# The first product of the output part cut into four row-tiled pieces inside the attention's last couple, in an attention and gated-FFN kernel on one core

## The chip, the cores and the metric

The kernel runs on one core of one Trainium2 chip. The metric is the device time of one execution in microseconds, lower is better. Times of the kernel before: 864.58 median of three runs (864.47 to 865.11).

## The reference

`x` is [1, 2048, 640]; there are 32 heads of 192 columns, and attention sees the last W = 512 rows of the caches. All inputs are bf16.

```python
xn = _layernorm(x)
q  = (xn @ wq) by heads;  k, v = the last 512 rows of k_cache, v_cache
p  = _softmax(q @ k.T * 192 ** -0.5)
s  = (p @ v, heads side by side: [2048, 6144]) @ wo          # wo: [6144, 640]
g  = _silu((_silu(xn @ w_gate) * (xn @ w_up)) @ w_down)
out = x + s * g
```

## The kernel before

The work runs in three parts. First the norm and the FFN, whose gate `g` is parked in DRAM (`g_d`). Then attention, 32 heads as 16 pairs, two pairs to a couple, four phases to a couple (32 phases in all); its outputs are transposed by DMA and parked in DRAM as `o_d`, by 16 tiles of 128 rows and 48 chunks of 128 head columns. Last the output part, `o @ wo` with the gate and the residual.

**A phase** handles two blocks of 512 query rows of one head pair. Its order on every engine is written by hand in a string of tokens, one string for each phase: `PHASES` for the common couples, `FIRST` and `LAST` for the first and last couple. `token()` turns each into instructions. A `<` in front means that the token belongs to the phase before, a `+` to the phase after. The tokens that matter here:

- `s0` to `s7` (`scores`, L1047): six matmuls of 64 rows by 512 columns into a pair of PSUM banks named `sc`, then one exponential on ACT (L1051) that writes `p_t`. There are two such pairs of banks, used in turn.
- `0a0`, `0a1`, `0b0`, `0b1`, `1a0` ... `1b1` (`context_unit`, `pv`, L1085): block 0 or 1, half a or b of it, first or second half of the unit: 16 matmuls of 193 columns, row-tiled: the lo and the hi 64 rows of the array work at the same time and write different banks. A digit after the point names the bank pair (`0` and `1` are `mm0` and `mm1`; `s` takes an `sc` pair). Between a unit's two halves the row tiles change banks, and the second half waits for a marker that POOL writes after the first (`turn_t`, L1063). After the second half DVE takes reciprocals (L1103) and scales into `O_b` (`O_last` for the last two blocks); a letter says who scales: `v` DVE alone (L1107), `a` ACT alone (L1113), none one half each. A DMA transpose on SP's queue follows, and `sp` (`spill`) writes the blocks to `o_d`.
- `RD RS RA RB RM RT` and the same with `J` (`q_group`, L990): products that make the next phase's q in groups of ten matmuls, with copies on ACT (`SIDE`, L1025), sums on DVE (L1028, L1038) and on POOL (L1032).
- `kc`, `kl`, `vl`, `wc` and others: k and v of the next couple; `bm0` to `bm3` (`b_sum`, L1165): quarters of the weight sum of M7; `as0`: its left-hand sum; `lA`, `lB` (`load_a`, L1178): a 768 KB quarter of `o_d` into `a_q` (A the first row pair, B the second; 0 to 3 are A11, A12, A21, A22); `xg`: rows of `x` and `g` for the end; `lM5`: a quarter of `wo`.

**The output part** takes the 16 row tiles in eight row pairs and computes each pair by seven products (a Strassen-like scheme, `M1` to `M7`) of 24 matmuls of 128 rows by 320 columns (`product`, L1201). `ORDER` interleaves the first two row pairs: M1 and M7 of pair 0, M1 and M7 of pair 1, then M2 of both, M5, M6, M4, M3; then the other pairs one by one. M7, M5, M6 and M3 take left-hand sums (`a_sum`, L1193, three buffers in rotation) and M7, M5, M6 and M4 weight sums (`b_sum`), all on DVE. M1 is copied out by ACT (`u`), M2 accumulates on top of M1's bank, and `finish` gates and adds the residual on DVE (L1222, L1223). SP issues all loads and stores in program order, and each waits for what it reads and overwrites, so a later load queues behind an earlier one that waits.

The last phase's token string, before:

```python
"s0 <0a1 <lA3 bm2 as0 s1 <1a0.1 s2 <1a1v s3 lB3 <1b0.0 s4 <1b1v s5 s6 <sp0 0a0.1 lB1 s7 0a1 bm3 0b0.s "
"0b1a 1a0.0 1b0.1 1a1a 1b1 <sp1 xg0",
```

Of the kernel before, what the change touches and what calls it, by code (L numbers as in the profile page):

```python
# [15 lines left out]
def kernel(  # L16
# [13 lines left out]
    nc = tc.nc  # L30
# [50 lines left out]
    def mm_tile(which=None):  # L81
        which = mm_next[0] if which is None else which
        mm_next[0] = 1 - which
        return mm_pool[0].tile([P, 2, 512], f32, name="mm", tag="mm%d" % which)
# [1084 lines left out]
    def load_a(n, q, cs=slice(0, KH), eng=nc.sync):  # L1169
        side, k = divmod(q, 2)  # L1170
        if (n, q) not in a_q:
            if n > 1:
                a_q[n, q] = a_q[n - 2, q]
            else:
                pool = pre if n == 0 and k == 0 else wide
                a_q[n, q] = pool.tile([P, KH, P], bf, name="a_q", tag="a_q%d%d" % (n, q))
        src = o_d[ROW_PAIRS[n][side], :, k * KH + cs.start : k * KH + cs.stop, :]
        eng.dma_start(out=a_q[n, q][:, cs, :], in_=src)  # L1178
# [16 lines left out]
    def product(n, m, ps, first=True):  # L1195
        at = a_s[n, m] if (n, m) in a_s else a_q[n, A_OF[m][0]]
        pss = ps if isinstance(ps, list) else [ps]
        w = HC // len(pss)
        for k, ps in enumerate(pss):
            for c in range(KH):  # L1200
                nc.tensor.matmul(  # L1201
                    ps[:, 0:w], at[:, c, :], b_w[m][:, c, k * w : (k + 1) * w],
                    start=(first and c == 0), stop=(c == KH - 1), skip_group_check=True,
                )
# [13 lines left out]
    def finish(n, side, k, s, in_psum=False):  # L1218

        t, cols = xg[n, side], slice(k * HC, (k + 1) * HC)  # L1220
        y = f_tile(n, 3) if in_psum else s
        nc.vector.tensor_tensor(y, s, t[:, 1, cols], ALU.mult)  # L1222
        nc.vector.tensor_tensor(t[:, 0, cols], y, t[:, 0, cols], ALU.add)  # L1223

    def store(n, side, cols=slice(0, D), eng=nc.sync):
        r = ROW_PAIRS[n][side]
        eng.dma_start(out=out2[r * P : (r + 1) * P, cols], in_=xg[n, side][:, 0, cols])

    V = nc.vector

    ORDER = [(n, m) for ms in ((M1, M7), (M2,), (M5,), (M6,), (M4,), (M3,)) for n in range(2) for m in ms]
    ORDER += [(n, m) for n in range(2, len(ROW_PAIRS)) for m in PRODUCTS]
    A_SUMS = [nm for nm in ORDER if len(A_OF[nm[1]]) == 3]

# [5 lines left out]
    def bank(n, name):  # L1240
        acc[n, name] = late[1].tile([P, 512], f32, name="acc")[:, 0:HC]
        return acc[n, name]

    def run(n, m):

        ahead = n + 2 < len(ROW_PAIRS)
        u, v, c = (f_tile(n, k) for k in range(3))
        if m == M1:
            ps = bank(n, "M1+M2")
            product(n, M1, ps)  # L1250
            nc.scalar.copy(u, ps)  # L1251
        elif m == M7:
            ps = bank(n, "M7+M4")
            product(n, M7, ps)
            nc.scalar.copy(v, ps)
        elif m == M2:
            ps = acc[n, "M1+M2"]
            product(n, M2, ps, first=False)
            finish(n, 0, 0, ps, in_psum=True)
            if (n, M3) == ORDER[-1]:  # L1260
                store(n, 0, slice(0, HC))
        elif m == M5:
            pss = [bank(n, "M5+M3"), bank(n, "M5+M3'")] if (n, M3) == ORDER[-1] else [bank(n, "M5+M3")]
            product(n, M5, pss)
            w = HC // len(pss)
            for k, ps in enumerate(pss):
                total(v[:, k * w : (k + 1) * w], ps[:, 0:w], v[:, k * w : (k + 1) * w])
        elif m == M6:
            ps = bank(n, "M6")
            product(n, M6, ps)  # L1270
            total(u, ps, u)
            total(v, u, v)
            finish(n, 1, 1, v)
            for q in (A11, A21) if ahead else ():
                load_a(n + 2, q)
        elif m == M4:
            ps = acc[n, "M7+M4"]
            product(n, M4, ps, first=False)
            total(c, ps, u)
            finish(n, 1, 0, c)  # L1280
            store(n, 1)
            if ahead:
                load_a(n + 2, A22)
        else:
            ps, t, last_cols = acc[n, "M5+M3"], xg[n, 0], slice(HC, D)
            if (n, m) == ORDER[-1]:
                total(u, u, t[:, 1, last_cols], ALU.mult)
                total(u, u, t[:, 0, last_cols])
                pss = [ps, acc[n, "M5+M3'"]]
                product(n, M3, pss, first=False)  # L1290
                w = HC // len(pss)
                for k, ps in enumerate(pss):
                    part, cols = slice(k * w, (k + 1) * w), slice(HC + k * w, HC + (k + 1) * w)
                    total(c[:, part], ps[:, 0:w], t[:, 1, cols], ALU.mult)
                    total(t[:, 0, cols], c[:, part], u[:, part])
                    store(n, 0, cols, (nc.sync, nc.scalar)[k])
            else:
                product(n, M3, ps, first=False)
                total(u, ps, u)
                finish(n, 0, 1, u)  # L1300
                store(n, 0)
            if ahead:
                load_a(n + 2, A12)
                load_xg(n + 2)
        if (n, m) in A_SUMS:
            k = A_SUMS.index((n, m)) + 3
            if k < len(A_SUMS):
                a_sum(*A_SUMS[k])

    FIRST = (  # L1310
# [20 lines left out]
    )  # L1331
    LAST = (
# [8 lines left out]
    )  # L1341
    COUPLES = NPAIR // 2
    PHASES_N = 4 * COUPLES
# [46 lines left out]
    def token(s, x):  # L1390
        nonlocal wide

        cp, ph = divmod(s, 4)
        if x[0].isdigit():
            context_unit(s, *x.split("."))
        elif x[0] == "s" and x[1].isdigit():
            scores(first_step(s) + int(x[1]) // KC, int(x[1]) % KC)
        elif x[:2] == "sp":
            spill(first_step(s) + int(x[2]))
        elif x[:2] in ("DG", "JG"):  # L1400
            q_diag(JOINT if x[0] == "J" else 1 if ph < 2 else 0, *x[2:])
        elif x[0] in "RJ":
            group_of(s, x[0])[x[1]](*x[2:])
        elif x[:2] in ("TT", "QQ"):
            k, j = (int(x[2]), 2) if x[0] == "T" else divmod(int(x[2]), 2)
            q_rows(first_step(s + 1) + k, j, int(x[3]))
        elif x == "ah":
            if s in AHEAD:
                what, *args = AHEAD[s]
                what(*args)  # L1410
        elif x[:2] == "vl":
            pr = 2 * cp + (1 if x[2] == "O" else 2 if s else 0)
            if pr < NPAIR:
                load_v(pr)
        elif x == "free":
            actx.close()
            wide = ctx.enter_context(tc.tile_pool(name="out_b", bufs=1, reuse_waits="tile"))
            O_last = wide.tile([P, 2, 4, 2, Dh], bf, name="O_last")
            O_late.extend(O_last[:, k, :, :, :] for k in range(2))
        elif x[:3] == "lM5":  # L1420
            n = int(x[3])
            load_b(M5, None, nc.sync, n * KH // 4, (n + 1) * KH // 4)
        elif x[0] == "l":
            load_a("AB".index(x[1]), int(x[2]))
        elif x[:2] == "xg":
            load_xg(int(x[2]))
        elif x[:2] == "bm":
            b_sum(M7, int(x[2]))
        elif x == "as0":
            a_sum(*A_SUMS[0])  # L1430
        else:
            what, n = (x[:-1], (int(x[-1]),)) if x[-1].isdigit() else (x, ())
            of_pair(s, what, n)
# [26 lines left out]
    for k, (n, m) in enumerate(ORDER):  # L1460
        run(n, m)
        for step in sums.get((n, m), ()):
            b_sum(*step)
        if k < 4:
            load_b(M3, late[0], nc.sync, k * KH // 4, (k + 1) * KH // 4)

# [29 lines left out]
```

## Time and profile before

| what | value |
|---|---|
| median of three runs | 864.58 us (864.47 to 865.11) |
| the profiled execution | 864.99 us; span of the core 863.2 us |
| granted clock of PE | 1.00 of full speed |
| busy share: PE, DVE, ACT, POOL | 99%, 71%, 54%, 19% |
| PE matmuls | 9805 recorded |
| DMA | 149.14 MB, mean 173 GB/s |
| first matmul of the output part | 677.10 us from the span's start |

The profile is of one execution. Times inside it count from the span's start. L1201 is line 1201 of the kernel; a group of instructions is named by its line, its engine, and what it writes and reads. "Idle before" is the idle time of that engine just before an instruction, and after the arrow stands who ended it. Matmul times are modelled to their end in the array, so two matmuls in flight overlap in the record.

### The profile page before, as it was taken

The numbers are of one execution on the slowest core, as the hardware profiler recorded it, in microseconds if no ns is written. First come the engines' busy times: TensorE is split into PE (matmuls) and PEld (weight loads), VectorE is DVE, ScalarE is ACT, GpSimd is POOL, SyncE is SP. The second block draws the span as 40 slices with busy tenths as digits, with TensorE's granted clock in tenths as the row PEclk, the third lists the DMA queues.
The fourth block names the chain that finished last, engine by engine and source line by source line (L and its number), as shares of the span: only waits on it lengthen the run. The fifth ranks groups of instructions, "written<-read, shape, count | busy, mean of one in ns | idle before, by whom it ended". The sixth has DMA issues, their size and how long they took to land.

```text
span 863.2 us, 23199 instructions
## 1 busy us (share of the span) xinstructions
PE 855.9 (99%) x9805; PEld 569.2 (66%) x9815; DVE 613.9 (71%) x1041; ACT 468.4 (54%) x644; POOL 167.0 (19%) x247
## 2 busy tenths in 40 slices
PE   8999999999999999999999999999999999999998
PEld 6456446576667667667667667667666777777776
DVE  6687987878777777777777777776755786565564
ACT  4474675667767767767767767767767400000000
POOL 0010000103333333333333333333321000000000
PEclk9999999999999999999999999999999999999999
DMA  9879413558877889989999978978998977645510
GB/s 294 174 143 212 72 40 107 132 93 164 183 143 167 195 164 204 222 160 208 208 171 195 230 135 173 196 167 194 155 227 230 265 250 232 236 154 182 174 46 17
DMA packets 271496, 149.14 MB, mean 173 GB/s; under 512 B 174112, under 2 KB 267296, under 8 KB 271392
## 3 DMA queue, kind: packets, MB, share of 16 engines
q1 hardware_dynamic: 270608, 147.01, 74.5%
q8 instruction: 77, 1.26, 0.6%
q10 hardware_dynamic: 784, 0.65, 0.3%
q14 instruction: 27, 0.22, 0.1%
HBM read 80.51 MB, written 30.41 MB: 128 GB/s over the span
## 4 chain that ended last, share of the span: by engine, by line
PE 98%; DMA 1%; ACT 0%; issue 0%; DVE 0%; SPq 0%; POOL 0%; ACTq 0%; POOLq 0%
PE acc L1201 21%; PE sc L1047 19%; PE mm L1085 14%; PE mm L990 12%; PE sc L990 7%; PE sc L394 5%; PE sc L1085 5%; PE mm L479 3%; PE mm L637 3%; PE sc L637 2%; PE sc L479 2%; PE mm L978 1%; PE sc L690 1%; DMA wg_sb<-in_B_w_gate_dram 1%; PE gu L394 0%
## 5 line engine op out<-in xcount | busy, mean ns | idle before, releaser
L1051 ACT ACTIVATE p_t<-sc 128x1024 bf16<-128x1024 f32 x256 | 258.2, 1023 | 89.4 <-PE sc L1047 88.4
L1047 PE MATMUL sc<-q_all,khat 64*128 64x512 bf16 x1536 | 206.4, 376 | 0.8 <-ACT O_b L1113 0.6
L1085 PEld LDWEIGHTS <-p_t 64*128 64x128 bf16 x4096 | 179.7, 94 | 36.6 <-POOL turn_t L1063 0.5
L1085 PE MATMUL mm<-V_p,p_t 64*128 64x193 bf16 x3008 | 157.4, 243 | 0.2
L990 PEld LDWEIGHTS <-w_all 64*128 64x128 f16 (+1 forms) x1540 | 86.2, 94 | 71.1 <-issue 0.5
L1047 PEld LDWEIGHTS <-khat 64*128 64x128 bf16 x1536 | 82.8, 94 | 56.4 <-issue 6.3
L1032 POOL TENSOR_TENSOR m_f<-m_f 128x1024 f32<-128x1024 f32 x44 | 105.3, 2394 | 42.4 <-DVE q_all L1028 28.4
L990 PE MATMUL mm<-xc,w_all 64*128 64x512 f16 x890 | 112.0, 376 | 0.0
L1028 DVE TENSOR_TENSOR q_all<-mm,m_f 128x1024 bf16<-128x1024 f32 x44 | 53.9, 1224 | 55.9 <-ACT m_f L1025 55.7
L1201 PE MATMUL acc<-b_w,a_q 128*128 128x320 bf16 (+1 forms) x576 | 81.8, 299 | 0.0
L1107 DVE TENSOR_TENSOR O_b<-mm,r 128x384 bf16<-128x384 f32 x151 | 78.3, 553 | 3.5 <-DVE r L1103 0.2
L1251 ACT COPY xc<-acc 128x320 f32<-128x320 f32 x8 | 3.4, 425 | 135.7 <-PE acc L1201 135.7
L1063 POOL MEMSET turn_t<- 128x1 f32 x128 | 12.7, 99 | 314.5 <-PE mm L1085 239.5
L1201 PEld LDWEIGHTS <-a_q 128*128 128x128 bf16 x576 | 56.3, 98 | 22.0 <-issue 0.2
L1201 PEld LDWEIGHTS <-q_all 128*128 128x128 f16 x552 | 52.7, 98 | 19.1
L1038 DVE TENSOR_TENSOR q_all<-mm,m_f 128x1024 bf16<-128x1024 f32 x44 | 53.7, 1220 | 12.2 <-POOL m_f L1032 5.9
L1201 PE MATMUL acc<-b_w,q_all 128*128 128x320 f16 (+2 forms) x432 | 58.1, 292 | 0.0
L1085 PE MATMUL sc<-V_p,p_t 64*128 64x193 bf16 x1088 | 53.7, 243 | 0.3 <-POOL turn_t L1063 0.3
L1103 DVE RECIPROCAL r<-mm 128x4 f32<-128x4 f32 x94 | 16.9, 179 | 51.0 <-PE mm L1085 50.8
L173 DVE TENSOR_TENSOR w_all<-wq_rows 64x640 f16<-64x640 bf16 x90 | 50.9, 617 | 0.5
L990 PE MATMUL sc<-xnT,w_all 64*128 64x512 bf16 x350 | 44.1, 376 | 0.0
L1025 ACT COPY m_f<-sc 128x1024 f32<-128x1024 f32 x35 | 35.4, 1012 | 13.3 <-PE sc L990 6.8
(173 smaller groups left out, 1028.5 us busy)
## 6 DMA issues: line engine op xcount, KB each, us to landing
o_d<-OT_b SPq DMA_DIRECT2D x64, 384.0 KB, 4.0
a_q<-o_d SPq DMA_DIRECT2D x32, 768.0 KB, 6.2
wq_rows<-in_A_wq_dram SPq DMA_DIRECT2D x16, 480.0 KB, 4.7
b_w<-in_A_wo_dram SPq DMA_DIRECT2D x16, 480.0 KB, 5.0
wq_rows<-in_A_wq_dram SPq DMA_DIRECT2D x30, 240.0 KB, 5.4
K_p<-in_A_k_cache_dram SPq DMA_DIRECT2D x32, 192.0 KB, 3.5
V_p<-in_A_v_cache_dram SPq DMA_DIRECT2D x32, 192.0 KB, 4.0
xc<-xnT SPq DMA_DIRECT2D x10, 320.0 KB, 4.6
```

The source lines that it names most:

```text
L173: nc.vector.tensor_tensor(slot_of(w_sum, r, at, to), x, y, op)
L394: nc.tensor.matmul(out, w_sb[:, c, f * P : (f + 1) * P], xnT[:, c, qc], start=(c == 0), stop=(c == NC - 1),)
L479: nc.tensor.matmul(ps, left[:, c, :], D_OF[m][:, c, :], start=(first and c == 0), stop=(c == KD - 1), skip_group_check=True,)
L990: nc.tensor.matmul(ps[:, h, :], ws[h][r, c, :], xs[h][r, c, :], start=(first and c == 0), stop=(c == NC - 1), skip_group_check=True,)
L1028: nc.vector.tensor_tensor(to[:, 1:3, :], st["ps"][:, :, :], m_f[:, 5:3:-1, :], ALU.add)
L1032: nc.gpsimd.tensor_tensor(SIDE, diag, SIDE, ALU.subtract)
L1038: nc.vector.tensor_tensor(to[:, 0:4:3, :], st["ps"][:, :, :], SIDE, ALU.add)
L1047: nc.tensor.matmul(sc[:, h, :], khat[r, j, ks], q_of(i, j)[r, :], start=(j == 0), stop=(j == 2))
L1051: nc.scalar.activation(p_t[:, :, :], sc[:, :, :], ACT.Exp, scale=scale)
L1085: m = nc.tensor.matmul(acc[:, k, h * 256 : h * 256 + Dh + 1], Ps[i][kc][r, h, qt * P : (qt + 1) * P], V_of[i // NB % 2][r, kc, h, 0 : Dh + 1],
L1107: nc.vector.tensor_tensor(O_b[:, k, :, :], a_k[:, :, 0:Dh], r[:, k, :, :].to_broadcast([P, 2, Dh]), ALU.mult,)
L1201: nc.tensor.matmul(ps[:, 0:w], at[:, c, :], b_w[m][:, c, k * w : (k + 1) * w], start=(first and c == 0), stop=(c == KH - 1), skip_group_ch ...
```

## The change

M1 of row pair 0 leaves `ORDER`. Its work is done by the new function `first_product`, in four pieces `o0` to `o3` among the last phase's scores and context units: six chunks a piece, each chunk as two matmuls of 64 rows (lo and hi) that write the two banks of `mm1`. After the last piece ACT copies one bank to `u`, and DVE adds the other. M2 of pair 0 gets a bank of its own instead of M1's, and `u` is added to it by DVE. All four token strings of the last couple are new: `vlO`, `lM5`, the `bm` sums, `xg1`, the `lA` and `lB` loads and the context units stand in other places and partly in other banks. In the output part the left-hand sum for (1, M5) is issued after M1 of pair 1 and its weight sums, and a later pair's A12 is loaded with A22 after M4, ahead of the store, not after M3.

```diff
--- before.py
+++ after.py
@@ -1228,7 +1228,7 @@
 
     V = nc.vector
 
-    ORDER = [(n, m) for ms in ((M1, M7), (M2,), (M5,), (M6,), (M4,), (M3,)) for n in range(2) for m in ms]
+    ORDER = [(n, m) for ms in ((M1, M7), (M2,), (M5,), (M6,), (M4,), (M3,)) for n in range(2) for m in ms][1:]
     ORDER += [(n, m) for n in range(2, len(ROW_PAIRS)) for m in PRODUCTS]
     A_SUMS = [nm for nm in ORDER if len(A_OF[nm[1]]) == 3]
 
@@ -1240,6 +1240,21 @@
     def bank(n, name):
         acc[n, name] = late[1].tile([P, 512], f32, name="acc")[:, 0:HC]
         return acc[n, name]
+
+    def first_product(part):
+
+        if part == 0:
+            acc[0, "M1"] = mm_tile(1)[:, :, 0:HC]
+        ps = acc[0, "M1"]
+        for c in range(part * KH // 4, (part + 1) * KH // 4):
+            for h, r in enumerate((lo, hi)):
+                nc.tensor.matmul(
+                    ps[:, h, :], a_q[0, A11][r, c, :], b_w[M1][r, c, :], start=(c == 0), stop=(c == KH - 1),
+                    skip_group_check=True,
+                )
+        if part == 3:
+            nc.scalar.copy(f_tile(0, 0), ps[:, 0, :])
+            total(f_tile(0, 0), ps[:, 1, :], f_tile(0, 0))
 
     def run(n, m):
 
@@ -1254,9 +1269,11 @@
             product(n, M7, ps)
             nc.scalar.copy(v, ps)
         elif m == M2:
-            ps = acc[n, "M1+M2"]
-            product(n, M2, ps, first=False)
-            finish(n, 0, 0, ps, in_psum=True)
+            ps = acc[n, "M1+M2"] if n else bank(n, "M2")
+            product(n, M2, ps, first=n == 0)
+            if n == 0:
+                total(f_tile(n, 3), ps, u)
+            finish(n, 0, 0, ps if n else f_tile(n, 3), in_psum=n > 0)
             if (n, M3) == ORDER[-1]:
                 store(n, 0, slice(0, HC))
         elif m == M5:
@@ -1278,9 +1295,9 @@
             product(n, M4, ps, first=False)
             total(c, ps, u)
             finish(n, 1, 0, c)
+            for q in (A12, A22) if ahead else ():
+                load_a(n + 2, q)
             store(n, 1)
-            if ahead:
-                load_a(n + 2, A22)
         else:
             ps, t, last_cols = acc[n, "M5+M3"], xg[n, 0], slice(HC, D)
             if (n, m) == ORDER[-1]:
@@ -1300,11 +1317,10 @@
                 finish(n, 0, 1, u)
                 store(n, 0)
             if ahead:
-                load_a(n + 2, A12)
                 load_xg(n + 2)
         if (n, m) in A_SUMS:
             k = A_SUMS.index((n, m)) + 3
-            if k < len(A_SUMS):
+            if 3 < k < len(A_SUMS):
                 a_sum(*A_SUMS[k])
 
     FIRST = (
@@ -1330,14 +1346,14 @@
         "1a0.1 <sp0",
     )
     LAST = (
-        "s0 ah RD kcO0 kcO1 kcO2 kcO3 s1 <1a1v RSs kcO4 s2 +++xg1 RA <sp0 <1b0.1 s3 RB <1b1 s4 vlO RM +++lM50 +++lM51 +++lM52 +++lM53 "
-        "RT s5 0a0.1 s6 0a1v s7 +RD +RSs 1a0.s 0b0.1 +RA +RB 1a1v 0b1v",
-        "s0 RM <<sp1 s1 s2 JD s3 RT JS0 <1b0.s ah ++bm0 s4 <1b1a JA 0a0.0 0b0.s 0a1 0b1 JB s5 <sp1 JM s6 +RD "
-        "JT s7 +RS1 ++bm1 <sp0 +RA",
-        "s0 <1a0.s ah <1b0.1 <sp0 <1a1 <1b1 s1 RB s2 RM free s3 lB2 s4 <sp1 0b0.1 RT lB0 s5 0b1v lA1 s6 s7 "
-        "0a0.0",
-        "s0 <0a1 <lA3 bm2 as0 s1 <1a0.1 s2 <1a1v s3 lB3 <1b0.0 s4 <1b1v s5 s6 <sp0 0a0.1 lB1 s7 0a1 bm3 0b0.s "
-        "0b1a 1a0.0 1b0.1 1a1a 1b1 <sp1 xg0",
+        "kcO0 kcO1 s0 <1a1v s1 kcO2 RD s2 RSs <sp0 RA <1b0.1 s3 <1b1v s4 RB vlO s5 kcO3 RM s6 0a0.1 s7 RT ah "
+        "0a1a kcO4 0b0.s +++lM50 +RD +RSs 0b1 1a0.1",
+        "s0 ah RA <1a1 s1 ++xg1 ++lM52 RB RM s2 RT JD JSs ++bm0 JA s3 ++lM53 <1b0.0 JB s4 <1b1v s5 <<sp1 JM "
+        "0a0.s JT s6 +RD <sp1 0a1 +RSs 0b0.1 ++lM51 s7 +RA",
+        "s0 RB <0b1v s1 RM <1b0.1 RT s2 s3 <1b1v ah <1a0.0 s4 <1a1v <<sp0 <sp0 +bm1 s5 0a0.1 s6 0a1v s7 free "
+        "0b0.0 <sp1",
+        "s0 <0b1v s1 <1a0.1 s2 <1a1 <1b0.0 s3 as0 <1b1v <lB0 o0 s4 s5 o1 <lB2 <lA3 0a0.0 <lA1 lB3 bm2 s6 o2 "
+        "s7 0b0.s xg0 o3 0b1a lB1 1a0.s <sp1 bm3 1b0.1 1a1v 1b1 <sp0 0a1a",
     )
     COUPLES = NPAIR // 2
     PHASES_N = 4 * COUPLES
@@ -1426,6 +1442,8 @@
             load_xg(int(x[2]))
         elif x[:2] == "bm":
             b_sum(M7, int(x[2]))
+        elif x[0] == "o":
+            first_product(int(x[1]))
         elif x == "as0":
             a_sum(*A_SUMS[0])
         else:
@@ -1461,6 +1479,8 @@
         run(n, m)
         for step in sums.get((n, m), ()):
             b_sum(*step)
+        if (n, m) == (1, M1):
+            a_sum(*A_SUMS[3])
         if k < 4:
             load_b(M3, late[0], nc.sync, k * KH // 4, (k + 1) * KH // 4)
```

## The prediction

> **What bounds the kernel now.** I read the page first, then PE's waits, then the engine timeline of the last couple, the chain there, and the windows around it.
>
> The page says that the time is PE's work with almost nothing between:
>
> ```profile
> PE 855.9 (99%) x9805; PEld 569.2 (66%) x9815; DVE 613.9 (71%) x1041; ACT 468.4 (54%) x644; POOL 167.0 (19%) x247
> PEclk9999999999999999999999999999999999999999
> PE 98%; DMA 1%; ACT 0%; issue 0%; DVE 0%; SPq 0%; POOL 0%; ACTq 0%; POOLq 0%
> ```
>
> An edit that leaves PE's work as it is can only win the time in which PE stands, and the windows say where that is near the change (columns: the stretch, its length, busy time of PE, PEld, DVE, ACT, POOL, then clock, DMA share, GB/s):
>
> ```profile
> 640.00:660.00 20.00, 19.22 (x290) 13.22 (x288) 8.81 (x14) 15.21 (x25) 5.24 (x8) 1.00 0.70 165
> 660.00:680.00 20.00, 19.55 (x318) 14.93 (x314) 11.87 (x22) 15.54 (x25) 0.69 (x7) 1.00 1.10 298
> 680.00:700.00 20.00, 20.00 (x149) 14.41 (x148) 17.31 (x17) 1.70 (x4) 0.00 (x0) 1.00 1.01 266
> ```
>
> The output part from 680 on is full; the couple before it loses 0.78 + 0.45 us. The true loss is larger, since a matmul's last stretch through the array counts as busy. So I measure from start to start, in the timeline of PE:
>
> ```profile
> 653.44 0.83 PE L1047 MATMUL sc<-q_all,khat 64*128 64x512 bf16 x6
> 654.91 0.82 PE L1047 MATMUL sc<-q_all,khat 64*128 64x512 bf16 x6 [0.64 <-ACT O_b L1113]
> 655.56 1.26 PE L990 MATMUL mm<-xc,w_all 64*128 64x512 f16 x10
> 658.01 1.16 PE L1085 MATMUL mm<-V_p,p_t 64*128 64x193 bf16 x16
> 659.00 0.81 PE L1047 MATMUL sc<-q_all,khat 64*128 64x512 bf16 x6
> 665.58 0.85 PE L1085 MATMUL mm<-V_p,p_t 64*128 64x193 bf16 x16
> 666.60 0.82 PE L1047 MATMUL sc<-q_all,khat 64*128 64x512 bf16 x6 [0.18 <-ACT p_t L1051]
> 672.54 0.84 PE L1085 MATMUL sc<-V_p,p_t 64*128 64x193 bf16 x16
> 673.66 0.84 PE L1085 MATMUL sc<-V_p,p_t 64*128 64x193 bf16 x16 [0.28 <-POOL turn_t L1063]
> 677.10 1.12 PE L1201 MATMUL acc<-b_w,a_q 128*128 128x320 bf16 x7
> ```
>
> Undisturbed, a block of scores (6 matmuls) takes 0.65 from its start to the next one's (654.91 to 655.56), half a context unit (16) 0.667 (32 in 1.33 us), ten products of L990 1.08. Against these the starts slip by 654.91 - 653.44 - 0.65 = 0.82; 659.00 - 658.01 - 0.667 = 0.32; 666.60 - 665.58 - 0.667 = 0.35; 673.66 - 672.54 - 0.667 = 0.45; and by 0.15 at 646.68, 0.07 at 657.3 and 0.10 at 677.10 (four halves from 674.34 end at 677.01). **Sum: 2.26 us.** The first four are a score that waits for ACT to empty its PSUM pair after a context unit had it; two that wait for an exponential held up behind ACT's O_b scaling; and a half that waits for POOL's turn marker because its sister half stands right before it.
>
> **The change, part by part.**
>
> *PE's work.* The same scores, halves and products of q remain, in another order. M1 of row pair 0 leaves the output part: 24 matmuls of 128 rows. Six M1, M7 and M2 products run from 677.10 to 696.67, so one costs 19.57/6 = 3.26 us, 136 ns a matmul. It comes back as 24 pairs of 64-row matmuls. No row shows such a pair at 320 columns; a pair of 193 columns takes 0.667/8 = 83.3 ns, one of 512 takes 0.647/3 = 215.8, and the straight line between gives 136.0 at 320. So 24 x 136.0 = 3.26: no change. Bounds: -0.1 and +0.2, from the fit; halves that do not overlap are excluded by both rows. That line leaves 3 ns for a pair beyond its columns, so 24 more matmul instructions cost under 0.1 us. The Trainium skill ("TensorEngine Tiling (Array Packing)", Instruction Overhead) speaks against such a split: it gives each matmul some 60 cycles of overhead. Read as time added, at its 2.4 GHz, that is an estimate of 24 x 25 ns = 0.6 us and a forecast of 863.5; the 193-column row, with 3 ns a pair, does not agree.
>
> *What fills the gaps.* The q.k bank rule can be read from the rows: a block of scores ends on PE 0.18 after its last issue, ACT starts 0.04 later, takes 1.02, and PE wakes 0.05 after that: 1.29 us from the end of one block to the start of the next on the same pair of banks. With two pairs, the other block (0.65) and one half (0.667) cover it with 0.02 to spare. An O_b scaling on ACT (0.73) between needs one half more. A piece of M1 is six pairs, 0.82 us of PE with nothing behind it for ACT or DVE: a better filler than a half. Walking the last phase as written: s6 stands 2.1 us behind s4; 0b0.s finds s6's exponential done after o2 and s7 (1.47 against 1.29: 0.18 to spare); o3 stands between 0b0 and 0b1, so POOL's 0.45 is covered; no score there waits. 0.35 + 0.45 go. In the three phases before, with the new order alone, I find two places that fall short, both round the SIDE copy of phase 29: s3 waits 0.11 for an sc pair that ACT's two O_b scalings (0.73) free late, and s4 then waits 0.26 for the copy (1.01) that stood behind them. So 0.15 + 0.82 + 0.07 + 0.32 go, and 0.37 come. The 0.10 at the first full product stays.
>
> *Late starts.* The chain shows delays of 0.25 to 0.5 with nothing to wait for:
>
> ```profile
> 653.64 0.49 issue
> 654.13 0.74 ACT O_b L1113 x2
> 664.03 0.24 issue
> 664.27 0.57 DVE O_b L1107
> ```
>
> With plain durations the old order's slips add up to 1.65; the other 0.6 are these. They hurt only where there is little to spare; the new order has eight such places (0.02 to 0.29). I take 0.1; bounds 0 and 0.6.
>
> *What is added.* ACT's copy of one half of M1 (0.42, the row of L1251) waits for o3, and O_last's scalings queue behind it; DVE's add (0.49, as L1222) waits for the copy, and behind it stand a reciprocal and the fourth M7 sum (1.15). 1b0 needs mm1 back: 0.22 + 0.43 + 0.54 + 0.05 = 1.24 after o3, against 1.33 for the two halves between. The M7 sum ends some 2.6 after o3; the first full product comes six halves (4.0) after. Nothing, if the 0.09 holds; if not, a tenth or two. M2 of pair 0 gets one more DVE add (0.49): DVE is free by the time, nobody waits.
>
> *The cover that goes.* The output part begins with M7, and M1's 3.26 no longer stand before the sums. DVE's a_sum for (1, M7) ended 2.5 us after 677.10; needed 6.5 after. M5's sums ended 8.5 after; needed 16.3. The a_sum for (0, M6) ended 16.1 after; needed 22.8. All covered.
>
> *Queues.* A12 of a row pair is loaded before the store and with A22, one product earlier than now: SP's order loosens. In the last couple SP gets five a_q loads in a row, xg of pair 0, a transpose of O_last, then the sixth a_q; before, the six lay between 659.39 and 672.73, among transposes. See the rivals.
>
> *Sum* against the profiled execution (864.99; span 863.2 and 1.8 around it): -2.26 + 0.10 + 0.37 + 0.1 = -1.69, so 863.30. The median of the runs shown is 0.41 under that execution: 864.58 - 1.69 = **862.9**.
>
> **The rivals.**
>
> *Forecast*: 862.9; with no late starts and the two new waits gone 862.3, with 0.6 of late starts and 0.2 on the pairs 863.6.
>
> *The order brings its own waits.* The pieces fill only the last phase, where 0.80 was lost; 1.36 lay before it, where only the new order acts. For: the margins there are down to 0.02. Against: the walk. Gain 0.8: 863.8.
>
> *A held pair of banks.* From o0 to the add M1 holds mm1, so context units fall on mm0 and sc. If 0b0.s and 1a0.s each make PE wait like the 0.82 at 654.91, the gain is gone: 864.58 - 1.69 + 1.64 = 864.5. The Trainium skill (the same page, Gotcha 1: PSUM Pressure) warns of this: row tiles must write different banks. The 0.82 row agrees that a held pair can stop PE; the 0.18 to spare speaks against it here.
>
> *Slower: the sixth load.* A12 of pair 1 (lB1) now stands on SP behind five loads, xg and a transpose. From the first of the five, some 8.1 us before the first full product (11.2 of PE work after 1b1v, less 3 for its scaling and transpose), 6 x 0.786 + 0.66 + 0.2 = 5.6 MB must come; M2 of pair 1 wants it 13.05 after that product begins, so 21.1 in all. That needs 265 GB/s. The window 660 to 680 had 298 (18.8: 2.3 to spare); 640 to 660 had 165, at a DMA share of 0.70, so not for want of rate. At 216, the rate of the window 620 to 640 (DMA share 1.05), it takes 25.9, PE waits 4.8, and the time is 867.7. It is slower than before from 246 GB/s down. For: the loads begin later than now. Against: the landing of a_q was 9.6 us at worst in that stretch.
>
> **How the numbers follow.** Forecast 0.72, own waits 0.10, held pair 0.06, sixth load 0.12. About 0.2% (1.73 us, to 862.85) is what a measurement of this kernel can tell. The forecast's 862.9 lies at that bound, with the late starts unsure either way: 0.40 of its 0.72 I put below. The rest, 0.32, and the two middle rivals are within: 0.48. Slower: 0.12. The range takes in the forecast's bounds and the two middle rivals, 862.3 to 864.8, and leaves out the sixth load.
>
> **What would show it.** PE's starts in the last couple without slips of 0.3 and more, its waits there under 0.6 in sum; o0 to o3 each 0.82; the first full product 1.6 later than now (3.26 more work, 1.69 less standing), with the output part at 136 ns a matmul and no DMA named among PE's waits. It is wrong if a piece takes over 0.9, if PE waits for ACT O_b round 0b0.s, or if M2 of pair 1 waits for a DMA.

## The result, and the profile after

The changed kernel takes 862.55 us (median of 11 runs, 862.2 to 864.85) against 864.51 for the kernel before (11 runs, 864.12 to 865.31). The ratio is 0.998 with a 95% interval of 0.9971 to 0.9989. The medians lie 2.0 us apart, and the interval means 1.0 to 2.5 us faster. One execution of a version tested below (`0a1v`) took 1118.41 us at a granted clock of 0.75; it counts as slow and is left out of that version's ratio.

In the windows of the profile after (the stretch, its length, then busy time of PE, PEld, DVE, ACT, POOL, the clock, DMA share, GB/s) the last couple's idle time of 1.23 us is down to 0.10:

```profile
640.00:660.00 20.00, 19.90 (x300) 13.91 (x297) 11.68 (x20) 13.66 (x16) 5.30 (x8) 1.00 0.82 177
660.00:680.00 20.00, 20.00 (x340) 16.23 (x335) 11.47 (x23) 12.83 (x21) 0.69 (x7) 1.00 1.06 258
680.00:700.00 20.00, 20.00 (x149) 14.41 (x148) 19.90 (x21) 2.21 (x6) 0.00 (x0) 1.00 1.00 261
```

PE's waits in the whole execution now lie in the opening of the FFN alone; none for ACT O_b, p_t or POOL's marker is left:

```profile
PE gu L323 <- DVE q_all L267: 1.2, 1, 1.2
PE sc L394 <- DMA wg_sb<-in_B_w_gate_dram: 0.4, 1, 0.4
PE sc L394 <- ACT xnT L742: 0.2, 1, 0.2
```

The timeline of PE in the profile after shows the pieces (L1251) among the last phase, start to start without a slip, and the first full product:

```profile
666.87 0.99 PE L1251 MATMUL mm<-b_w,a_q 64*128 64x320 bf16 x12
667.68 1.48 PE L1047 MATMUL sc<-q_all,khat 64*128 64x512 bf16 x12
668.98 0.99 PE L1251 MATMUL mm<-b_w,a_q 64*128 64x320 bf16 x12
669.79 0.85 PE L1085 MATMUL mm<-V_p,p_t 64*128 64x193 bf16 x16
...
673.24 0.99 PE L1251 MATMUL mm<-b_w,a_q 64*128 64x320 bf16 x12
674.05 1.51 PE L1085 MATMUL sc<-V_p,p_t 64*128 64x193 bf16 x32
...
676.72 1.51 PE L1085 MATMUL mm<-V_p,p_t 64*128 64x193 bf16 x32
678.16 3.43 PE L1201 MATMUL acc<-b_w,q_all 128*128 128x320 f16 x24
```

A piece costs 667.68 - 666.87 = 0.81 us. Slips, counted as in the prediction from start to start, remain in three places: 0.20 at 648.45, 0.26 at 649.36, and 0.11 at the first full product. Sum 0.57, against 2.27 before (2.26 in the prediction, by rounding): 1.70 less. From the first full product to the end the kernel before took 863.2 - 677.1 = 186.1 us and the changed one 861.0 - 678.2 = 182.8, which is one product less and nothing else. So the other edits of the output part neither won nor lost time that can be seen here.

The span fell by 2.2 (863.2 to 861.0). Most of what the slips leave over lies ahead of the attention: the first 50 us, which the change does not touch, happen to have 0.4 more of PE busy (48.07 against 47.66), and the first exponential starts at 160.8 instead of 161.2. In the nine profiled executions of this document it starts between 160.2 and 161.2, latest in the kernel before, though none of the edits touches that part: this share of the gain is chance.

The two slips of 0.20 and 0.26 are one story, told by PE (first fence), DVE and ACT (second):

```profile
645.84 0.85 PE L1085 MATMUL sc<-V_p,p_t 64*128 64x193 bf16 x16
646.50 1.26 PE L990 MATMUL sc<-xnT,w_all 64*128 64x512 bf16 x10
647.58 0.84 PE L1085 MATMUL mm<-V_p,p_t 64*128 64x193 bf16 x16
648.45 1.73 PE L1047 MATMUL sc<-q_all,khat 64*128 64x512 bf16 x12
```

```profile
646.72 0.18 DVE L1103 RECIPROCAL r<-sc 128x4 f32<-128x4 f32 x1 [1.45 <-PE sc L1085]
646.94 0.56 DVE L1107 TENSOR_TENSOR O_b<-sc,r 128x384 bf16<-128x384 f32 x1
647.67 0.73 ACT L1113 ACTIVATE O_b<-sc,r 128x192 bf16<-128x192 f32 x2 [1.61 <-DVE O_b L1107]
648.29 1.01 ACT L1025 COPY m_f<-sc 128x1024 f32<-128x1024 f32 x1
649.31 1.02 ACT L1051 ACTIVATE p_t<-sc 128x1024 bf16<-128x1024 f32 x1
```

A context unit in an `sc` pair issues its last matmul just ahead of 646.50. Its scaling is split, one half on DVE and one on ACT, but the two run one after the other: DVE's half ends at 647.50, and ACT, which had been idle for 1.61 us, starts at 647.67. (In all 33 split units of this trace in which ACT stood idle when DVE's half ended, ACT began 0.08 to 0.17 behind that end.) So the pair is free only at 648.40, and the score due at 648.25 starts at 648.45. ACT's copy of the q product, behind that scaling, frees the other pair at 649.30, and the score due at 649.10 starts at 649.36.

SP's queue shows the six loads of `a_q` (first and last line) and the transpose ahead of the sixth:

```profile
670.19 2.84 SPq L1178 DMA_DIRECT2D a_q<-o_d  x5
...
677.17 4.36 SPq L1116 DMA_TRANSPOSE OT_b<-O_last  x1
681.58 0.63 SPq L1178 DMA_DIRECT2D a_q<-o_d  x1
```

The sixth landed at 689.82, and M2 of pair 1, which reads it, began at 691.21.

### The profile page after: what moved, and what is told of

It reads as the page before. It is cut to its first block, busy times and chain, and to the rows that moved or that the text cites. A ratio compares the mean times of both kernels' runs of the same rounds, so it can differ in the third digit from the quotient of the medians.

```text
span 861.0 us, 23263 instructions
## 1 busy us (share of the span) xinstructions
PE 855.7 (99%) x9839; PEld 569.5 (66%) x9839; DVE 616.8 (72%) x1046; ACT 466.7 (54%) x638; POOL 166.8 (19%) x247
## 4 chain that ended last, share of the span: by engine, by line
PE 98%; DMA 1%; ACT 0%; DVE 0%; SPq 0%; issue 0%; ACTq 0%
PE acc L1201 21%; PE sc L1047 19%; PE mm L1085 15%; PE mm L990 12%; PE sc L990 7%; PE sc L394 6%; PE sc L1085 5%; PE mm L479 3%; PE mm L637 3%; PE sc L637 2%; PE sc L479 2%; PE mm L978 1%; PE sc L690 1%; DMA wg_sb<-in_B_w_gate_dram 1%; PE gu L394 0%; PE mm L1251 0%
## 5 line engine op out<-in xcount | busy, mean ns | idle before, releaser
L1107 DVE TENSOR_TENSOR O_b<-mm,r 128x384 bf16<-128x384 f32 x155 | 80.3, 553 | 3.2
L1201 PE MATMUL acc<-b_w,a_q 128*128 128x320 bf16 (+1 forms) x552 | 78.4, 299 | 0.0
L1201 PEld LDWEIGHTS <-a_q 128*128 128x128 bf16 x552 | 54.0, 98 | 21.0
L1085 PE MATMUL sc<-V_p,p_t 64*128 64x193 bf16 x1056 | 51.9, 243 | 0.0
L990 PE MATMUL sc<-xnT,w_all 64*128 64x512 bf16 x370 | 46.6, 376 | 0.0
L1025 ACT COPY m_f<-sc 128x1024 f32<-128x1024 f32 x37 | 37.5, 1012 | 13.8 <-PE sc L990 7.3
```

Of the source, the lines that this page charges most:

```text
L990: nc.tensor.matmul(ps[:, h, :], ws[h][r, c, :], xs[h][r, c, :], start=(first and c == 0), stop=(c == NC - 1), skip_group_check=True,)
L1085: m = nc.tensor.matmul(acc[:, k, h * 256 : h * 256 + Dh + 1], Ps[i][kc][r, h, qt * P : (qt + 1) * P], V_of[i // NB % 2][r, kc, h, 0 : Dh + 1],
L1107: nc.vector.tensor_tensor(O_b[:, k, :, :], a_k[:, :, 0:Dh], r[:, k, :, :].to_broadcast([P, 2, Dh]), ALU.mult,)
L1201: nc.tensor.matmul(ps[:, 0:w], at[:, c, :], b_w[m][:, c, k * w : (k + 1) * w], start=(first and c == 0), stop=(c == KH - 1), skip_group_ch ...
```

## The experiments

"Slips" below are summed as above, over the last couple and the first product after it, in one profiled execution of each kernel. The kernel before has 2.27, the changed one 0.57. Slips recur: the pair of 0.20 and 0.26 stands in five of the kernels here, each time within 0.02 us. Ratios are to the kernel before, measured alongside. Of the versions that alter the changed kernel, only the one with the sixth load later has an interval clear of the changed kernel's; for the others the slips have to tell them apart.

**The new order without the pieces.** The kernel before with the four new strings, `o0` to `o3` left out (shown: the last phase's string):

```diff
-        "s0 <0a1 <lA3 bm2 as0 s1 <1a0.1 s2 <1a1v s3 lB3 <1b0.0 s4 <1b1v s5 s6 <sp0 0a0.1 lB1 s7 0a1 bm3 0b0.s "
-        "0b1a 1a0.0 1b0.1 1a1a 1b1 <sp1 xg0",
+        "s0 <0b1v s1 <1a0.1 s2 <1a1 <1b0.0 s3 as0 <1b1v <lB0 s4 s5 <lB2 <lA3 0a0.0 <lA1 lB3 bm2 s6 "
+        "s7 0b0.s xg0 0b1a lB1 1a0.s <sp1 bm3 1b0.1 1a1v 1b1 <sp0 0a1a",
```

> The kernel before with the new strings of the last couple alone, o0 to o3 taken out; M1 of pair 0 stays a full product in the output part. Theory 'order and pieces need each other': the two waits of the changed kernel round the SIDE copy stay (0.46 us), and without fillers the last phase walks to 1.7: s4 or s5 0.15 behind ACT's O_b scaling, 0a0 0.5 for DVE's scaling of 1b out of mm0, 0b0.s 0.65 for the exponential of s6 (0.65 of PE between instead of 1.29), 0b1 0.4 for POOL's marker right behind 0b0. Slips 2.2 to 2.4 in all, as many as before: 864.3 to 864.9, no gain. Rival 'the order wins by itself what lay ahead of the last phase': the last phase loses the old 0.8, slips 1.3: 863.5.

Measured: 864.38, the kernel before alongside 864.35, ratio 1.0001 (0.9992 to 1.001). Slips 2.30: the two of the changed kernel (0.20 and 0.25), then 0.14, 0.45, 0.70 and 0.46 in the last phase, 0.10 at the first product. In its timeline of PE:

```profile
668.50 0.84 PE L1085 MATMUL mm<-V_p,p_t 64*128 64x193 bf16 x16 [0.27 <-DVE O_b L1107]
669.17 1.46 PE L1047 MATMUL sc<-q_all,khat 64*128 64x512 bf16 x12
671.16 0.84 PE L1085 MATMUL sc<-V_p,p_t 64*128 64x193 bf16 x16 [0.53 <-ACT p_t L1051]
672.28 1.51 PE L1085 MATMUL sc<-V_p,p_t 64*128 64x193 bf16 x32 [0.28 <-POOL turn_t L1063]
```

The order alone wins nothing: what it saves ahead of the last phase (1.36 down to 0.45) it gives back there (0.80 up to 1.75).

**The pieces without the new order.** The changed kernel with the old strings, and in the last phase (a cut of the string):

```diff
-... <1b1v s5 s6 <sp0 0a0.1 lB1 s7 0a1 bm3 0b0.s 0b1a 1a0.0 ...
+... <1b1v o0 s5 s6 o1 <sp0 0a0.0 lB1 s7 o2 0a1 bm3 0b0.s o3 0b1a 1a0.0 ...
```

> The changed kernel with the old strings of the last couple, and o0 to o3 put into its last phase: o0 ahead of s5, o1 after s6, o2 after s7, o3 between 0b0 and 0b1. Theory 'order and pieces need each other': the fillers take away 0.45 (POOL's marker) and 0.2 to 0.35 at s5, the 1.36 ahead of the last phase stay: slips 1.5 to 1.75, 863.7 to 863.9. Rival 'the pieces are the whole gain': slips about 0.6, 862.6. Rival 'a held pair of banks costs': a new wait for ACT O_b or DVE in the last phase, 864.5 or more.

Measured: 863.98, ratio 0.9998 (0.9989 to 1.0007). Slips 1.82: POOL's 0.46 is gone, since `o3` now stands between the two halves (674.00 and 675.48), and all else is as before. One part missed: the 0.35 stayed, because that score is `s3` (665.65), and I put `o0` behind `s4`:

```profile
665.65 0.82 PE L1047 MATMUL sc<-q_all,khat 64*128 64x512 bf16 x6 [0.18 <-ACT p_t L1051]
666.30 0.84 PE L1085 MATMUL mm<-V_p,p_t 64*128 64x193 bf16 x16
666.96 0.83 PE L1047 MATMUL sc<-q_all,khat 64*128 64x512 bf16 x6
667.61 0.84 PE L1085 MATMUL mm<-V_p,p_t 64*128 64x193 bf16 x16
668.28 0.99 PE L1251 MATMUL mm<-b_w,a_q 64*128 64x320 bf16 x12
...
674.00 0.85 PE L1085 MATMUL sc<-V_p,p_t 64*128 64x193 bf16 x16
674.66 0.99 PE L1251 MATMUL mm<-b_w,a_q 64*128 64x320 bf16 x12
675.48 0.84 PE L1085 MATMUL sc<-V_p,p_t 64*128 64x193 bf16 x16
```

Both halves of the change together save 1.70; alone they save nothing and 0.45. The pieces are what lets the new order run.

**The pieces as full matmuls.** The changed kernel, M1 in the same four places but 128 rows high:

```diff
-            for h, r in enumerate((lo, hi)):
-                nc.tensor.matmul(
-                    ps[:, h, :], a_q[0, A11][r, c, :], b_w[M1][r, c, :], start=(c == 0), stop=(c == KH - 1),
+            nc.tensor.matmul(
+                ps[:, 0, :], a_q[0, A11][:, c, :], b_w[M1][:, c, :], start=(c == 0), stop=(c == KH - 1),
...
-            total(f_tile(0, 0), ps[:, 1, :], f_tile(0, 0))
```

> The changed kernel with M1's four pieces as full matmuls of 128 rows (six a piece, one bank, no DVE add) in the same places. Theory 'a change between 64-row and 128-row matmuls costs the 0.10 that stands at the first full product': eight such changes more, slips up by 0.8 from 0.6 to 1.4: 863.3, each piece 0.82 and about 0.1 lost ahead of it and behind it. Rival 'row tiling is beside the point, only the filler counts': slips as in the changed kernel, 862.5. Rival 'the split into 24 more matmuls costs 0.6': faster by up to 0.6, 862.0, pieces of 0.65 to 0.8.

Measured: 863.38, ratio 0.9988 (0.9979 to 0.9996). Slips 1.41. PE's waits name nobody in the last couple; the loss is round each piece, in the timelines of PE and of its weight loads (PEld):

```profile
665.55 0.85 PE L1085 MATMUL mm<-V_p,p_t 64*128 64x193 bf16 x16
666.33 0.99 PE L1250 MATMUL mm<-b_w,a_q 128*128 128x320 bf16 x6
667.25 1.47 PE L1047 MATMUL sc<-q_all,khat 64*128 64x512 bf16 x12
```

```profile
666.32 0.66 PEld L1250 LDWEIGHTS <-a_q 128*128 128x128 bf16 x6 [0.16 <-issue]
667.24 0.76 PEld L1047 LDWEIGHTS <-khat 64*128 64x128 bf16 x10 [0.26 <-issue]
```

From 665.55 a half ends its issue at 666.22, the piece starts at 666.33; its six matmuls (0.815) end their issue at 667.14, the scores start at 667.25: 0.11 each way. Over the eight changes it is 0.09 to 0.11 each, and the slips grow by 0.84. So the row tiling is worth that much, and the 0.11 at the first full product has the same size. The first weight load behind a change starts only with its matmul (666.32 and 666.33), and what holds it the profile doesn't name ("issue"). In the changed kernel the piece's first weight load starts at 666.79, 0.08 ahead of its matmul at 666.87. The Trainium skill ("TensorEngine Tiling (Array Packing)", Key Properties) says that a change of tiling mode drains the engine. The trace agrees with that as far as it goes: nothing of the next block starts early, and each change costs about 0.1 us.

**The two waits that are left.** The changed kernel with one token changed in the second string:

```diff
-... 0a0.s JT s6 +RD <sp1 0a1 +RSs 0b0.1 ...
+... 0a0.s JT s6 +RD <sp1 0a1v +RSs 0b0.1 ...
```

> The changed kernel with one token changed: unit 0a in an sc pair of the phase before the last but one is scaled by DVE alone, so that ACT's two O_b scalings (0.73) leave the way of the SIDE copy. Theory 'the two waits left come from ACT's O_b scaling in that queue': both go, slips 0.6 to 0.15, 862.1. Rival 'DVE becomes late instead': its two scalings (1.02 and a reciprocal of 0.18) free the sc pair later than ACT did, PE waits for DVE there, 862.5 or more.

Measured: 862.12, ratio to the kernel before 0.9976 (0.9966 to 0.9985). Slips 0.13, nearly all of it at the first full product. In the timelines of PE, DVE and ACT the two scores run without a gap:

```profile
647.88 0.84 PE L1085 MATMUL mm<-V_p,p_t 64*128 64x193 bf16 x16
648.54 1.48 PE L1047 MATMUL sc<-q_all,khat 64*128 64x512 bf16 x12
```

```profile
647.01 0.18 DVE L1103 RECIPROCAL r<-sc 128x4 f32<-128x4 f32 x1 [1.45 <-PE sc L1085]
647.23 1.02 DVE L1107 TENSOR_TENSOR O_b<-sc,r 128x384 bf16<-128x384 f32 x2
648.09 1.01 ACT L1025 COPY m_f<-sc 128x1024 f32<-128x1024 f32 x1 [1.74 <-PE sc L990]
```

The copy starts 0.20 earlier than in the changed kernel (648.29), though PE is 0.30 later here, so 0.50 earlier against PE's work. The rival failed because a split unit is not scaled side by side: DVE alone frees the pair 648.25 - 647.01 = 1.24 after its reciprocal begins, while half and half it took 648.40 - 646.72 = 1.68.

This version has the lowest median of all. Its interval overlaps the changed kernel's; that it is better by some 0.4 rests on the slips in the profile.

**The sixth load, later.** The changed kernel with `lB1` at the end of the last phase:

```diff
-... xg0 o3 0b1a lB1 1a0.s <sp1 bm3 1b0.1 1a1v 1b1 <sp0 0a1a
+... xg0 o3 0b1a 1a0.s <sp1 bm3 1b0.1 1a1v 1b1 <sp0 0a1a lB1
```

> The changed kernel with the sixth a_q load (A12 of pair 1) moved to the end of the last phase, so that it stands on SP behind all four O_last transposes. In the trace of the changed kernel it was issued at 681.58, landed at 689.82, and M2 of pair 1 began at 691.21: 1.4 us to spare; the fourth transpose was issued at 690.59 and took 1.42. Theory 'that load is the next thing to be late': issued about 691.3, landing 4 to 5 later, PE waits 3.5 to 5 ahead of M2 of pair 1 and nothing gives it back: 866.0 to 867.5, slower than before. Rival 'the DMA queues catch up': the transposes ahead go through sooner without the load between them, it lands by 692.5 and the wait is under 1.3: 862.5 to 863.8.

Measured: 867.68 (865.9 to 870.31), ratio 1.0032 (1.0018 to 1.0047): slower than before, and 0.2 above the upper end of what I expected. The profile is of the slowest of the eight executions, 870.31. There the load was issued at 691.98 and landed at 696.90; M2 of pair 1 was due at 692.69. In the timeline of PE, and in windows round it:

```profile
689.43 3.42 PE L1201 MATMUL acc<-b_w,a_q 128*128 128x320 bf16 x24
696.95 5.11 PE L1201 MATMUL acc<-b_w,a_q 128*128 128x320 bf16 x24 [4.09 <-DMA a_q<-o_d]
701.89 3.29 PE L1201 MATMUL acc<-xc,a_s 128*128 128x320 f16 x23
```

```profile
694.00:698.00 4.00, 1.05 (x8) 0.79 (x9) 3.93 (x5) 0.00 (x0) 0.00 (x0) 0.99 0.97 345
698.00:702.00 4.00, 4.00 (x19) 2.35 (x18) 0.15 (x1) 0.00 (x0) 0.00 (x0) 0.58 0.79 218
702.00:706.00 4.00, 4.00 (x32) 2.87 (x30) 2.63 (x5) 0.00 (x0) 0.00 (x0) 1.00 1.17 322
```

The wait, 696.95 - 692.69 = 4.3, lies where it was expected. What was not: the product behind it took 701.89 - 696.95 = 4.94 instead of 3.26, and the window 698 to 702 has a granted clock of 0.58. The slow stretch is not its start: the matmuls from 697.9 to 701.3 stand 267 ns apart, those ahead and behind 136. The Trainium skill ("TensorE: Matmul & The Clock Gate", Part 1) has the clock fall to half after an idle window of about 3.4 us and rise again after as long. The trace agrees: the slow stretch is 3.4 us long at half the pace, which makes the 1.7 us lost. A further 1.4 us of this execution is a wait for DVE ahead of the last couple, so 4.3 + 1.7 + 1.4 = 7.4 explain nearly all of the 7.5 that it has over the profiled execution of the changed kernel (862.80). The median is lower, so not every execution lost all of this; which part the others lost, no trace shows.

**The sixth load, earlier.** The version with `0a1v` and `lB1` ahead of `xg0`:

```diff
-... s7 0b0.s xg0 o3 0b1a lB1 1a0.s ...
+... s7 0b0.s lB1 xg0 o3 0b1a 1a0.s ...
```

> The version with unit 0a scaled by DVE alone, with the sixth a_q load issued as the sixth in the row, ahead of xg and of the first O_last transpose. Theory 'a load that is early enough costs and wins nothing': it lands about 686 instead of 689.8, M2 of pair 1 gets some 5 us to spare instead of 1.4, the time stays at 862.1. Rival 'six in a row push the others out': the a_q quarters that the sums of pair 1 want land later and PE waits for DVE ahead of M7 of pair 1: 862.5 or more.

Measured: 862.72 (861.89 to 865.06), ratio 0.9977 (0.9968 to 0.9986). Slips 0.13. The load landed at 688.53 and M2 of pair 1 was due at 693.44: 4.9 to spare, and no time won. That execution was 2.0 behind the changed kernel's at the row's first load, so the landing is where it was expected, and nobody waited for the others. The median stands 0.6 over that of the version it starts from, but the kernel before stood 0.2 higher as well (864.59 against 864.35), and the two ratios are the same, 0.9977 and 0.9976. So no difference is shown. The profiled execution (865.02) lost 2.7 us at two scores ahead of 600 us, in a part that this edit does not touch.

**The held pair of banks.** The changed kernel with 1b0 (in `mm1`) one half behind `o3`, not two:

```diff
-... o3 0b1a lB1 1a0.s <sp1 bm3 1b0.1 1a1v 1b1 <sp0 0a1a
+... o3 0b1a lB1 1b0.1 <sp1 bm3 1a0.s 1b1 1a1v <sp0 0a1a
```

> The changed kernel with the last units' order changed so that 1b0, which needs mm1 back from M1, stands one half (0.667 us) behind o3 instead of two. In the trace of the changed kernel DVE's add ended 1.17 us after o3's last issue (674.05 to 675.22). Theory 'the held pair of banks has 0.1 to spare, as in the walk': PE waits 0.5 to 0.6 for DVE there: slips 0.6 to 1.15, 863.1. Rival 'the next half finds other banks or the release comes earlier': no new wait, 862.5.

Measured: 863.1, ratio 0.9985 (0.9977 to 0.9994). Slips 1.11; the new one in the timeline of PE:

```profile
673.76 0.84 PE L1085 MATMUL sc<-V_p,p_t 64*128 64x193 bf16 x16
674.98 0.84 PE L1085 MATMUL mm<-V_p,p_t 64*128 64x193 bf16 x16 [0.37 <-DVE xc L1238]
```

674.98 - 673.76 - 0.667 = 0.55, and the profile names DVE's add. This unit stood 0.667 later in the changed kernel, so 0.667 - 0.55 = 0.1 was to spare there.

## Why the prediction was right

- *Slips, the term that carries the sum.* 1.69 was forecast, 1.70 measured; the old ones went as listed. That the agreement is to 0.01 is partly luck, as the next item shows.
- *New waits.* 0.11 and 0.26 were forecast, 0.20 and 0.26 came, for the cause given: two O_b scalings on ACT, then the SIDE copy behind them. What the prediction does not spell out is that ACT's scalings are late because they start behind DVE's half. The 0.09 more is such a start: ACT began 0.17 behind DVE's half here (647.50 to 647.67), where at 665.96 it began 0.08 behind. The prediction's term for late starts (0.1, bounds 0 and 0.6) covers it; it was taken, not worked out, so its fit is luck. But I put the wrong names to them: the two scores are `s7` of the second string and `s0` of the third, and the copy belongs to the next phase's q. The walk had the engines and times right and the tokens wrong; a mistake of the same kind put `o0` in the wrong place in the experiment with the pieces alone.
- *A piece* was priced 0.82 and took 0.81, 135 ns a pair: the straight line from the rows of 193 and 512 columns held. The estimate of 0.6 us for 24 more matmuls, from the Trainium skill ("TensorEngine Tiling (Array Packing)", Instruction Overhead), did not show: six full matmuls and six pairs both take 0.81.
- *Row tiling.* The prediction never weighed it against pieces of full matmuls, which cost 0.84 more in slips.
- *The first full product* came 1.06 later, not 1.6: the forecast had no term for the 0.4 that came ahead of the attention in that execution, by chance, and that is most of the difference.
- *Held pair*: a margin of 0.09 was forecast; the experiment that took 0.667 from it made PE wait 0.55, so it was 0.1. PE waited at neither `0b0.s` nor `1a0.s`, the two places that this rival named.
- *The sixth load* was a live risk. It landed 19.6 us after the first of the row was issued (670.19 to 689.82), against 18.8 forecast, and M2 of pair 1 had 1.4 to spare, not 2.3. Divided out, 5.6 MB in 19.6 us is 285 GB/s against the 298 I took, but that is not a rate at which this load moved. It was issued only at 681.58, 11.4 us after the first, since the transpose ahead of it took 4.36 us of SP's queue. Issued as the sixth in a row, in the experiment with the load earlier, it landed 16.3 us after the first (672.22 to 688.53). Moved later, the same load made the kernel slower than before, by PE's wait ahead of M2 of pair 1 that this rival foresaw. The reason was its place in SP's queue, though, not the low rate that the rival priced: once issued it landed in 4.9 us. And a part of the loss (1.7 in the profile) came by the clock, which the rival did not price. The prediction also says that before the change the six loads began at 659.39; the first of them was issued at 657.49.
- *The 0.2% bound.* 862.9 was forecast, 862.55 came, just beyond the bound on the faster side; nearly half of the interval lies within. The slips account for 1.70 of the 1.96 between the medians; the rest is within the interval and is not explained.

## What to carry to other kernels

Where PE is 99% busy, measure its losses from start to start against undisturbed blocks of the same kind, and walk the new order with those blocks: where the tokens were placed right, that told each wait within 0.1 us. A filler is worth what it keeps from the other engines: M1's pieces bring PE work with nothing for ACT or DVE behind it, and only with them does the better order pay. Give a filler the row tiling of the matmuls around it. A scaling split between two engines frees a bank sooner only if the two halves run side by side, which the trace has to show. After every move of loads, count what now queues ahead of the last of them.

## What the runs showed of the hardware

- A change between 64-row and 128-row matmuls costs PE about 0.1 us, though no wait names it: 0.09 to 0.11 at each of the eight changes round the full pieces, 0.10 to 0.12 at the first full product of all nine kernels.
- In the profiled execution with the sixth load later, a wait of PE of 4.3 us cost 6.0: the next product of 24 matmuls took 4.94 us instead of 3.26, with matmuls 267 ns apart instead of 136 for 3.4 us of it, and a granted clock of 0.58 over the window 698 to 702.
